# Seven turned block products with wh for three of four pairs of blocks, and wh's pieces made in the first mixing layer

## The chip, the cores and the metric

The kernel runs on one core of a Trainium2 chip. The metric is the device time of one execution in microseconds: 1596.6 us before, the median of 3 runs (1596.59 to 1599.89).

## What is computed

Four layers work on x, 2048 rows of 512 numbers in f32. Layers 0 and 2 mix: a two-sided discrete Fourier transform of the normalized rows, of which the real part is kept. Layers 1 and 3 are a gated feed-forward block. Each adds to x.

```python
def _A_ref(x, dft_seq_re, dft_seq_im, dft_hid_re, dft_hid_im):
    a = jnp.einsum("bsd,ed->bse", x, dft_hid_re)
    b = jnp.einsum("bsd,ed->bse", x, dft_hid_im)
    y = jnp.einsum("ts,bse->bte", dft_seq_re, a) - jnp.einsum("ts,bse->bte", dft_seq_im, b)
    return y

def _B_ref(x, w_gate, w_up, w_down):
    return (_gelu(x @ w_gate) * (x @ w_up)) @ w_down

x = x + _A_ref(_layernorm(x, axis=-1), A_dft_seq_re, A_dft_seq_im, A_dft_hid_re, A_dft_hid_im)
x = x + _B_ref(_layernorm(x, axis=-1), B_w_gate, B_w_up, B_w_down)
...
```

The kernel multiplies in the other order: first the transform over the sequence (ws), then the one over the 512 columns (wh).

## The kernel before

**Products.** TensorE (PE) takes f32 values as pairs of a high and a low part: ScalarE (ACT) copies the high part (L157), VectorE (DVE) subtracts it for the low part (L159), and `mm3` (L214 to L216) makes three matmuls of 128x512. The parts of the streamed matrices are made on the fly: `take` hands out the next item of a list `items`, and makes parts for up to seven items ahead.

**Fewer products by sums.** A product of 2x2 blocks of matrices is made with seven products instead of eight, from sums and differences of the blocks. That is done for ws, for the gate and up matrices and mostly for the down matrix. Sums are VectorE's work (`plus` L194 and L197, `minus` L190).

**A mixing layer** (`mix`) goes through four blocks of 512 rows. `plan` lists the steps: A11 and A12 of all blocks, then for each block S2 (144 matmuls: three products, for which VectorE makes three sums and three low parts for each k), wh products, S4 (96 matmuls) and the other wh products. With wh a block has eight products of 12 matmuls (`hid_groups`): two before S4 (EARLY_HID), six behind it (MID_HID, LATE_HID). Their results lie in four banks, which ScalarE seeds with x and copies out.

**A pair** (`pair_groups`, `pair_product`). Two blocks can share seven products with wh, turned: wh's piece is the stationary operand, and the results are columns. Then wh stands as seven pieces (`whd`), made from whc by `weight_steps`: sums and four `divide` steps, with VectorE, ScalarE and stores on GpSimd's (POOL) queue. Each of the seven products P1 to P7 has four values of k, and six matmuls for each. The blocks' sums are differences of their columns: `arrived` (P7 and P5), `pair_sums` (P6 and P3). Results are added on VectorE and turned by `turned_into` (a transpose L815 and a sum L197 into a wide tile that holds x). The first block of a pair has 2 products before S4 and 6 behind it, the second also; the remaining twelve (PAIR_REST: P6, P5 and P3) come later. Before, only blocks 2 and 3 of layer 2 are a pair, and its rest stands in layer 3, one product at a time beside the up products (`spare`, `beside_mix`). wh's pieces are made in the second half of layer 1.

**Chores.** Work for later layers (norms, weights' pieces) is cut into small steps, spread over the wh products: `chores_at` says which block has which.

**Order.** The order of each engine's instructions follows from the program's order, priorities and a scheduler; each engine then takes its instructions in that order. Slots `s` are 98 tiles of 128x512 in SBUF, to which 8 more are lent from the wide tiles `wide` and `xwide` while these are free (`lend`, `reclaim`); `p` are 8 banks of PSUM.

Of the kernel before, what the change touches and what calls it, by code (L numbers as in the profile page):

```python
# [17 lines left out]
ND = D // P  # L18
# [25 lines left out]
MIXED = 4  # L44
PAIRED = {2: (2, 3)}
LATER = 3
LET = 5
# [6 lines left out]
def fnet_geglu(ctx: ExitStack, tc: tile.TileContext, x_in, ws, wh, wgu, wdn, wdc, whc, out):  # L54
# [409 lines left out]
    )  # L464
    PAIR_REST = [(name, k) for name in ("P6", "P5", "P3") for k in (2, 3, 0, 1)]
# [12 lines left out]
    def plan(layer):  # L478

        fore, steps = FORE[layer], []  # L480
        steps += [(b, "A11") for b in range(fore)] + [(b, "A12") for b in range(fore)]
        for b in range(NB):
            if b >= fore:
                steps += [(b, "A11"), (b, "A12")]
            if b in PAIRED.get(layer, ()):
                n = PAIRED[layer].index(b)
                steps += [(b, "S2"), (b, PAIR_EARLY[n]), (b, "S4"), (b, PAIR_LATE[n])]
            else:
                steps += [(b, "S2"), (b, EARLY_HID), (b, "S4"), (b, MID_HID), (b, LATE_HID)]
        return steps  # L490
# [23 lines left out]
    def mix_items(layer):  # L514
# [3 lines left out]
        for b, what in plan(layer):  # L518
# [17 lines left out]
            elif what == "S4":  # L536
                for i, k in skewed(2):
                    if layer and (b, k) in wss and i == 0:
                        raw(plain, wss[b, k][3])
                    elif i == 0:  # L540
                        raw(make_s4(layer, b, k), a12[k])
                    else:
                        raw(plain, a22[k])
            elif b in PAIRED.get(layer, ()):
# [277 lines left out]
    def mix(layer):  # L822
        hid, sums, chores, hid_left = {}, {}, [], [0]

        def chores_at(b):
            if b == NB - 3:
                norms, others = block_steps(layer + 1, 0)
                later.update(norms=norms[NT:], fetches=others[:ND], others=others[ND:])
                return norms[:NT]
            if b == NB - 2:  # L830
# [35 lines left out]

        paired = PAIRED.get(layer, ())
        xu, xv, pair_banks, kept_p, pair_wide, late_v, sums_due = {}, {}, {}, {}, {}, {}, []

        def arrived(b, m, c):  # L870
            if b not in paired:
                return
            t = cs.pop((m, c))
            if b == paired[0]:
                (xv if m else xu)[c] = t
                cs["P2" if m else "P1", c] = t
                return
# [19 lines left out]

        def pair_wide_load(n):
# [3 lines left out]
            moved(pair_wide[n], xs[layer, paired[n]], lambda v, rows: nc.sync.dma_start(v, rows))  # L902

        def pair_out(n):
            moved(pair_wide[n], xs[layer + 1, paired[n]], lambda v, rows: nc.gpsimd.dma_start(rows, v))

# [153 lines left out]
        def s2(b):  # L1060
            last = b == NB - 1
            if b == 0:
                lend("z")
# [39 lines left out]
        def s4(b):  # L1103
            last = b == NB - 1
            if b == NB - 4:
                sb.reclaim("z")
            if paired and b == paired[0] - 1:
                sb.reclaim("x")
# [160 lines left out]
    def geglu(w, layer):  # L1269
# [517 lines left out]
```

## Time and profile before

| | |
|---|---|
| median of 3 runs | 1596.6 us |
| profiled execution, span | 1596.4 us |
| instructions | 22835 |
| DMA | 431.75 MB, mean 270 GB/s |
| matmuls of L214, L215, L216 | 2312 each |

The span lies 0.2 us below the median, so sums are made on the span. In the trace, the blocks of layer 0 follow each other from 97 us on, about 76 us each, until 402 us; layer 1 lasts until 802 us, layer 2's blocks begin at 889 us, and layer 3 at about 1174 us. A busy PE in the profile is modelled, so what it can lose is read from the starts of matmuls, and from what they wait for. The numbers 0 to 3 of layers and blocks are the code's.

### The profile page before, as it was taken

To read this page: it belongs to the slowest core of one execution; us is meant where nothing else is said; L and a number is where in the kernel's file an instruction comes from. 1 tells how busy PE (TensorE), PEld (TensorE's weight loads), DVE (VectorE), ACT (ScalarE), POOL (GpSimd) and SP (SyncE) were. 2 spreads that over 40 slices of the span, in tenths; PEclk is the share of its full clock that TensorE was granted. 3 is DMA by queue.
4 is the path that set the end of the run, shared out by engine and by line. 5 is a ranking of instruction groups with operands and counts; after the bars stand their busy time and mean duration, and the time that the engine had idled before them with its cause. 6 is when DMAs were issued, how large, how long until landed. Compare 5 with 4: busy or idle time off the path is not lost.

```text
span 1596.4 us, 22835 instructions
## 1 busy us (share of the span) xinstructions
PE 1590.0 (100%) x6984; PEld 1311.2 (82%) x6984; DVE 1169.2 (73%) x2030; ACT 891.6 (56%) x1731; POOL 294.9 (18%) x505
## 2 busy tenths in 40 slices
PE   9999999999999999999999999999999999999999
PEld 6888888888888888888888888888888888888887
DVE  7997878888689794665879767778895557844574
ACT  8955465755777553666657535556553565333460
POOL 4122111251456101330040000101301000000000
PEclk9999999999999999999999999999999999999999
DMA  9898888996988999997895876878978958895445
GB/s 352 289 336 310 292 319 274 359 315 201 324 317 321 285 319 295 332 363 239 288 303 177 272 248 215 272 239 256 254 258 275 284 182 253 300 291 175 133 145 158
DMA packets 244058, 431.75 MB, mean 270 GB/s; under 512 B 29344, under 2 KB 68512, under 8 KB 242912
## 3 DMA queue, kind: packets, MB, share of 16 engines
q1 hardware_dynamic: 214128, 337.21, 66.2%
q0 software_dynamic: 27120, 90.99, 15.7%
q10 hardware_dynamic: 2688, 2.10, 0.5%
q8 instruction: 55, 0.90, 0.2%
q14 instruction: 67, 0.55, 0.1%
HBM read 341.31 MB, written 88.87 MB: 269 GB/s over the span
## 4 chain that ended last, share of the span: by engine, by line
PE 91%; issue 3%; DMA 3%; DVE 2%; ACT 1%; POOL 1%; SPq 0%; DVEq 0%; POOLq 0%; ACTq 0%
PE p L214 30%; PE p L215 30%; PE p L216 30%; DVE s L159 1%; DMA s<-ws 1%; DMA s<-t 1%; PE p L1010 0%; ACT s L157 0%; DMA s<-x 0%; DVE s L190 0%; POOL rstd L628 0%; DMA wide<-ws 0%; POOL s L754 0%; DVE xwide L190 0%; POOL wb L323 0%
## 5 line engine op out<-in xcount | busy, mean ns | idle before, releaser
L215 PE MATMUL p<-s,s 128*128 128x512 f32 x2312 | 897.4, 389 | 0.8 <-DVE s L159 0.8
L216 PE MATMUL p<-s,s 128*128 128x512 f32 x2312 | 891.8, 389 | 0.0
L214 PE MATMUL p<-s,s 128*128 128x512 f32 x2312 | 860.4, 389 | 0.3 <-ACT p L208 0.2
L157 ACT ACTIVATE s<-s 128x512 fp32r<-128x512 f32 (+1 forms) x855 | 481.3, 608 | 265.3 <-DVE s L190 73.6
L159 DVE TENSOR_TENSOR s<-s,s 128x512 fp32r<-128x512 f32 (+1 forms) x855 | 536.6, 661 | 115.3 <-ACT s L157 97.7
L215 PEld LDWEIGHTS p<-s,s 128*128 128x128 f32 x2312 | 433.9, 188 | 91.9 <-DVE s L159 1.9
L214 PEld LDWEIGHTS p<-s,s 128*128 128x128 f32 x2312 | 433.9, 188 | 91.7 <-ACT p L208 0.9
L216 PEld LDWEIGHTS p<-s,s 128*128 128x128 f32 x2312 | 434.0, 188 | 90.3
L194 DVE TENSOR_TENSOR s<-s,p 128x512 f32<-128x512 f32 x201 | 135.6, 682 | 160.3 <-PE p L216 138.1
L190 DVE TENSOR_TENSOR s<-s,s 128x512 f32<-128x512 f32 (+1 forms) x413 | 243.5, 609 | 6.2 <-DMA s<-ws 2.8
L201 ACT ACTIVATE s<-p 128x512 f32<-128x512 f32 x232 | 134.3, 593 | 108.0 <-PE p L216 106.3
L1264 ACT ACTIVATE s<-s 128x512 f32<-128x512 f32 x84 | 52.8, 628 | 46.4 <-DVE s L194 45.5
L628 POOL TENSOR_SCALAR rstd<-rstd 128x1 f32<-128x1 f32 x40 | 19.6, 489 | 237.2 <-ACT s L627 229.3
L1264 ACT ACTIVATE s<-p 128x512 f32<-128x512 f32 x28 | 16.7, 598 | 83.2 <-PE p L216 81.6
L323 POOL DMA_DIRECT2D wb<-s x84 | 46.1, 550 | 92.7 <-ACT s L157 70.5
L159 DVE TENSOR_TENSOR s<-xwide,s 128x512 fp32r<-128x512 f32 (+1 forms) x52 | 34.9, 679 | 29.2 <-ACT s L157 29.2
L651 ACT ACTIVATE s<-s,shift,rstd 128x512 f32<-128x512 f32 x59 | 47.5, 812 | 15.2 <-DVE shift L618 8.5
L1280 DVE TENSOR_TENSOR s<-s,p 128x512 f32<-128x512 f32 x56 | 38.2, 683 | 23.7 <-PE p L216 23.7
L197 DVE TENSOR_TENSOR s<-s,s 128x512 f32<-128x512 f32 (+1 forms) x71 | 42.8, 609 | 11.9 <-DMA s<-ws 10.4
L208 ACT ACTIVATE p<-p 128x512 f32<-128x512 f32 x56 | 32.6, 585 | 24.0 <-PE p L216 23.7
L157 ACT ACTIVATE s<-xwide 128x512 fp32r<-128x512 f32 (+1 forms) x52 | 31.6, 622 | 25.5 <-DVE xwide L194 18.2
L1201 POOL DMA_DIRECT2D wc<-s x42 | 30.5, 728 | 70.8 <-ACT s L157 61.9
(104 smaller groups left out, 614.9 us busy)
## 6 DMA issues: line engine op xcount, KB each, us to landing
s<-ws SPq DMA_DIRECT2D x404, 256.0 KB, 5.2
s<-wb SPq DMA_DIRECT2D x294, 256.0 KB, 5.2
s<-wc SPq DMA_DIRECT2D x182, 256.0 KB, 4.7
wb<-s POOLq DMA_DIRECT2D x98, 256.0 KB, 4.9
s<-wh SPq DMA_DIRECT2D x84, 256.0 KB, 5.3
s<-x SPq DMA_DIRECT2D x55, 256.0 KB, 5.4
wc<-s POOLq DMA_DIRECT2D x49, 256.0 KB, 5.3
xwide<-ws SPq DMA_DIRECT2D x37, 256.0 KB, 5.3
```

The costliest lines, as they stand in the source:

```text
L157: newest["ACT"] = nc.scalar.activation(hi, src, AF.Copy)
L159: newest["DVE"] = nc.vector.tensor_tensor(lo, src, f32(hi), op=ALU.subtract)
L190: nc.vector.tensor_tensor(out, a, b, op=ALU.subtract)
L194: bank_read["DVE"] = nc.vector.tensor_tensor(out, a, b, op=ALU.add)
L197: nc.vector.tensor_tensor(out, a, b, op=ALU.add)
L201: bank_read["ACT"] = nc.scalar.activation(v, src, AF.Copy)
L214: nc.tensor.matmul(ps, ah, bh, start=start, stop=False, skip_group_check=True)
L215: nc.tensor.matmul(ps, ah, bl, start=False, stop=False, skip_group_check=True)
L216: newest["PE"] = nc.tensor.matmul(ps, al, bh, start=False, stop=stop, skip_group_check=True)
L323: nc.gpsimd.dma_start(a, f32(t))
L651: nc.scalar.activation(z, x, AF.Identity, bias=shift, scale=rstd)
L1264: nc.scalar.activation(t, g, AF.Gelu_apprx_tanh)
```

## The change

Three of the four pairs of blocks in the two mixing layers now take seven turned products: blocks 2 and 3 of layer 0, and both pairs of layer 2; blocks 0 and 1 of layer 0 keep eight products each. Four `weight_steps` for wh's pieces move from layer 1 into the chores of blocks 0 and 1 of layer 0. The rest of layer 0's pair stands beside the up products of layer 1, that of layer 2's second pair as before in layer 3; that of layer 2's first pair (`PAIR_REST`) is a step of its own behind block 1, ahead of S2 of block 2. In layer 2, where block 0 is paired, the wide tiles aren't lent in the blocks, and the norms of the first four row tiles for layer 3 move from block 1 to block 2.

```diff
-PAIRED = {2: (2, 3)}
-LATER = 3
+PAIRED = {0: ((2, 3),), 2: ((0, 1), (2, 3))}
+LATER = 4
...
+    def paired_with(layer, b):
+        return next((p for p in PAIRED.get(layer, ()) if b in p), ())
...
-            if b in PAIRED.get(layer, ()):
-                n = PAIRED[layer].index(b)
+            if paired_with(layer, b):
+                n = paired_with(layer, b).index(b)
                 steps += [(b, "S2"), (b, PAIR_EARLY[n]), (b, "S4"), (b, PAIR_LATE[n])]
+                if n and b < NB - 1:
+                    steps.append((b, PAIR_REST))
...
         def chores_at(b):
+            jobs = []
+            if layer == 0 and paired and b < ND // 2:
+                two = [weight_steps(k, whc, whd) for k in range(2 * b, 2 * b + 2)]
+                jobs = [two[0][0]] + [run for i, (_, runs) in enumerate(two) for run in [load for load, _ in two[i + 1:]] + runs]
+            return jobs + next_layer(b)
+
+        def next_layer(b):
             if b == NB - 3:
                 norms, others = block_steps(layer + 1, 0)
-                later.update(norms=norms[NT:], fetches=others[:ND], others=others[ND:])
-                return norms[:NT]
+                later.update(norms=norms if b in paired else norms[NT:], fetches=others[:ND], others=others[ND:])
+                return [] if b in paired else norms[:NT]
...
         def pair_groups(b, groups):
-            n, early = paired.index(b), groups in PAIR_EARLY
+            pair_now[0] = by_pair[b]
+            n, early = by_pair[b].index(b), groups in PAIR_EARLY
+            if groups is PAIR_REST:
+                for i in range(len(groups)):
+                    pair_rest(i)
+                    step()
...
+                return
             if early:
                 chores.extend(chores_at(b))
-                hid_left[0] = 16 if n else 8
-                if not n:
-                    fetch_sums(paired[1])
-                pair_wide_load(n)
+                hid_left[0] = 16 if n and b == NB - 1 else 20 if n else 8
+                if b + 1 < NB:
+                    fetch_sums(b + 1)
+                pair_wide_load(b, n)
             for i, (name, k) in enumerate(groups):
-                if not early and not n and i == 2:
-                    s2_seeded(paired[1])
+                if not early and b + 1 < NB and i == (4 if n else 2):
+                    s2_seeded(b + 1)
...
-                spare.extend(lambda i=i: pair_rest(i) for i in range(len(PAIR_REST)))
+                if b == NB - 1:
+                    spare.extend(lambda i=i: pair_rest(i) for i in range(len(PAIR_REST)))
...
+            if layer and first_paired == 0 and b == FORE[layer] - 1:
+                sb.reclaim("x")
+                sb.reclaim("z")
...
-            if b == 0:
+            if b == 0 and first_paired:
                 lend("z")
                 lend("x")
...
-            run = spare.pop(0) if spare and (layer > 1 or n >= 1) else None
+            run = spare.pop(0) if spare and (w == 0 or n >= 1) else None
...
-            jobs = [weight_steps(k, whc, whd) for k in range(ND)]
+            jobs = [] if 0 in PAIRED else [weight_steps(k, whc, whd) for k in range(ND)]
```

**Layer 2, the end of block 1's S4.** VectorE's rows before, as built: the last two sums from S4's banks `p3` and `p6`, then sums of ws for S2 of block 2 (L197, L190) and the parts of wh products (L185, L159).

```order
L194 TENSOR_TENSOR s61_11180<-s61_11180,p3_10942 128x512
L194 TENSOR_TENSOR s31_11182<-s31_11182,p6_10943 128x512
L197 TENSOR_TENSOR s57_11508<-s79_11506,s57_11508 128x512
L197 TENSOR_TENSOR s20_11518<-s71_11516,s20_11518 128x512
L197 TENSOR_TENSOR s47_11560<-s86_11558,s47_11560 128x512
L197 TENSOR_TENSOR s78_11609<-s55_11607,s78_11609 128x512
L185 SCALAR_TENSOR_TENSOR s6_11555<-s61_11180,s15_11554 128x512
L190 TENSOR_TENSOR s79_11506<-s5_11510,s79_11506 128x512
```

VectorE's rows of the change at the same place: four sums from S4's banks (L194) with the pair's differences between and behind them.

```order
L194 TENSOR_TENSOR s55_11465<-s11_11202,p2_10966 128x512
L194 TENSOR_TENSOR s25_11467<-s0_11204,p5_10967 128x512
L190 TENSOR_TENSOR s21_11469<-s20_10802,s55_11465 128x512
L190 TENSOR_TENSOR s35_11472<-s23_10804,s25_11467 128x512
L190 TENSOR_TENSOR s55_11465<-s55_11465,s96_11245 128x512
L190 TENSOR_TENSOR s25_11467<-s25_11467,s78_11247 128x512
L159 TENSOR_TENSOR s50_11478<-s21_11469,s22_11477 128x512
L159 TENSOR_TENSOR s47_11484<-s35_11472,s53_11483 128x512
L194 TENSOR_TENSOR s11_11202<-s11_11202,p1_10968 128x512
L194 TENSOR_TENSOR s0_11204<-s0_11204,p0_10969 128x512
L190 TENSOR_TENSOR s20_10802<-s55_11465,s20_10802 128x512
L190 TENSOR_TENSOR s23_10804<-s25_11467,s23_10804 128x512
```

The sums of ws for the next block's S2, which stood right behind S4's last sums, now stand some forty rows further on, behind the differences and sums of the pair.

**Layer 0, from S4 of block 2 to S2 of block 3.** VectorE's rows before: the last sums of S4, sums of ws, and the sums of 256 that belong to a piece of the gate and up matrices.

```order
L194 TENSOR_TENSOR s26_3363<-s26_3363,p1_3102 128x512
L194 TENSOR_TENSOR s88_3365<-s88_3365,p2_3103 128x512
L197 TENSOR_TENSOR s20_3719<-xwide_1457,s20_3719 128x512
L197 TENSOR_TENSOR s22_3729<-s62_3727,s22_3729 128x512
L197 TENSOR_TENSOR s48_3461<-s27_3462,s48_3461 128x256
L190 TENSOR_TENSOR s68_3460<-s79_3459,s27_3462 128x256
L185 SCALAR_TENSOR_TENSOR s15_3766<-s26_3363,s85_3765 128x512
```

VectorE's rows of the change there, from the last two sums of S4 on.

```order
L194 TENSOR_TENSOR s31_3488<-s31_3488,p1_3233 128x512
L745 STREAM_TRANSPOSE wide_3648<-s55_3912 128x16x32
L194 TENSOR_TENSOR s79_3490<-s79_3490,p2_3234 128x512
L197 TENSOR_TENSOR s85_3838<-s17_3836,s85_3838 128x512
L159 TENSOR_TENSOR s90_3853<-s24_3834,s35_3852 128x512
L197 TENSOR_TENSOR s3_3848<-s22_3846,s3_3848 128x512
L197 TENSOR_TENSOR s72_3591<-s18_3592,s72_3591 128x256
L190 TENSOR_TENSOR s89_3590<-s34_3589,s18_3592 128x256
L185 SCALAR_TENSOR_TENSOR s48_3879<-s31_3488,s80_3878 128x512
```

A transpose of the norms and a part for a wh product have come between the same kinds of rows; behind them PE has 36 matmuls with wh ahead of block 3's S2, where it had 72.

**Layer 2, the end of block 3's S4.** VectorE's rows of the change, with the bank that the first product of layer 3 takes over, `p1`.

```order
L194 TENSOR_TENSOR s55_13195<-s0_12906,p7_12630 128x512
L194 TENSOR_TENSOR s22_13197<-s25_12908,p6_12631 128x512
L190 TENSOR_TENSOR s61_13223<-s42_12860,s73_13161 128x512
L159 TENSOR_TENSOR s9_13232<-s96_13129,s56_13231 128x512
L159 TENSOR_TENSOR s58_13242<-s73_13161,s14_13241 128x512
L190 TENSOR_TENSOR s12_13199<-s8_12371,s55_13195 128x512
L194 TENSOR_TENSOR s0_12906<-s0_12906,p1_12632 128x512
```

PE's rows there: the last matmuls of S4, and behind them the first product of layer 3, into `p1`.

```order
L215 MATMUL p7_12630<-s52_13094,s88_9478 128x512
L216 MATMUL p7_12630<-s92_13093,s88_9478 128x512
L215 MATMUL p6_12631<-s52_13094,s88_9478 128x512
L216 MATMUL p6_12631<-s92_13093,s88_9478 128x512
L214 MATMUL p1_13381<-s5_12997,s18_13249 128x512
L215 MATMUL p1_13381<-s7_12998,s18_13249 128x512
```

VectorE's rows before at that place begin with sums from `p2` and `p0`.

```order
L194 TENSOR_TENSOR s33_12740<-s33_12740,p2_12466 128x512
L190 TENSOR_TENSOR s42_13029<-s42_13029,s93_12781 128x512
L194 TENSOR_TENSOR s47_12742<-s47_12742,p0_12467 128x512
L159 TENSOR_TENSOR s65_13134<-s23_12965,s20_13133 128x512
L159 TENSOR_TENSOR s76_13168<-s30_12910,s38_13167 128x512
```

Before, the other two banks of S4 had been read some 20 matmuls earlier; now all four end together, and the sum that frees `p1` is VectorE's seventh row behind them.

More of the change, by code (lines that the diff above doesn't have):

```diff
@@ L464, in fnet_geglu @@
     )
-    PAIR_REST = [(name, k) for name in ("P6", "P5", "P3") for k in (2, 3, 0, 1)]
+    PAIR_REST = tuple((name, k) for name in ("P6", "P5", "P3") for k in (2, 3, 0, 1))
     def pair_items(names):
         return [(F32R, (piece(whd[k], FORM[name]),), make_pair(name, k), (name, k)) for name, k in names]
+    def paired_with(layer, b):
+        return next((p for p in PAIRED.get(layer, ()) if b in p), ())
     def skewed(n):
@@ L543, in mix_items @@
                         raw(plain, a22[k])
-            elif b in PAIRED.get(layer, ()):
+            elif paired_with(layer, b):
                 items.extend(pair_items(what))
@@ L865, in hid_groups @@
                     x_out(layer, b * NT + i, ps)
-        paired = PAIRED.get(layer, ())
-        xu, xv, pair_banks, kept_p, pair_wide, late_v, sums_due = {}, {}, {}, {}, {}, {}, []
+        paired = {b for p in PAIRED.get(layer, ()) for b in p}
+        first_paired = min(paired, default=NB)
+        by_pair = {b: p for p in PAIRED.get(layer, ()) for b in p}
+        xu, xv, pair_banks, kept_p, pair_wide, late_v, sums_due, pair_now = {}, {}, {}, {}, {}, {}, [], [()]
         def arrived(b, m, c):
@@ L873, in arrived @@
             t = cs.pop((m, c))
-            if b == paired[0]:
+            if b == by_pair[b][0]:
                 (xv if m else xu)[c] = t
@@ L896, in pair_sums, with pair_wide_load @@
             cs["P6", c], cs["P3", c] = u, v
-        def pair_wide_load(n):
+        def pair_wide_load(b, n):
             pool = tpool if n else upool
@@ L901, in pair_wide_load @@
             pair_wide[n] = pool.tile([P, NT * D], F32, name="wide" if n else "xwide")
-            moved(pair_wide[n], xs[layer, paired[n]], lambda v, rows: nc.sync.dma_start(v, rows))
+            moved(pair_wide[n], xs[layer, b], lambda v, rows: nc.sync.dma_start(v, rows))
         def pair_out(n):
-            moved(pair_wide[n], xs[layer + 1, paired[n]], lambda v, rows: nc.gpsimd.dma_start(rows, v))
+            moved(pair_wide[n], xs[layer + 1, pair_now[0][n]], lambda v, rows: nc.gpsimd.dma_start(rows, v))
         LAST = {"P1": 3, "P2": 1, "P7": 3, "P4": 1, "P6": 1, "P5": 1, "P3": 1}
@@ L959, in pair_groups @@
         def pair_groups(b, groups):
-            n, early = paired.index(b), groups in PAIR_EARLY
+            pair_now[0] = by_pair[b]
[4 more added lines that the diff above has]
+                    step()
+                    for _ in range(-(-len(chores) // hid_left[0]) if chores else 0):
+                        chores.pop(0)()
+                    hid_left[0] -= 1
+                return
             if early:
                 chores.extend(chores_at(b))
-                hid_left[0] = 16 if n else 8
-                if not n:
-                    fetch_sums(paired[1])
-                pair_wide_load(n)
+                hid_left[0] = 16 if n and b == NB - 1 else 20 if n else 8
+                if b + 1 < NB:
+                    fetch_sums(b + 1)
+                pair_wide_load(b, n)
             for i, (name, k) in enumerate(groups):
-                if not early and not n and i == 2:
-                    s2_seeded(paired[1])
+                if not early and b + 1 < NB and i == (4 if n else 2):
+                    s2_seeded(b + 1)
                 pair_product(name, k)
@@ L1104, in s4 @@
             last = b == NB - 1
-            if b == NB - 4:
+            if b == NB - 4 and first_paired:
                 sb.reclaim("z")
-            if paired and b == paired[0] - 1:
+            if b == first_paired - 1:
                 sb.reclaim("x")
```

## Prediction

> **What bounds the kernel now.** First the page's busy line and the chain of work that ended last: is one engine the wall, or several by turns?
>
> ```profile
> PE 1590.0 (100%) x6984; PEld 1311.2 (82%) x6984; DVE 1169.2 (73%) x2030; ACT 891.6 (56%) x1731; POOL 294.9 (18%) x505
> PE 91%; issue 3%; DMA 3%; DVE 2%; ACT 1%; POOL 1%; SPq 0%; DVEq 0%; POOLq 0%; ACTq 0%
> ```
>
> TensorE holds 91% of the chain. A busy share of 100% is not yet proof, so the second view is the list of waits, for PE alone:
>
> ```profile
> PE p L1693 <- POOL ident masks.py:199: 1.4, 1, 1.4
> PE p L215 <- DVE s L159: 0.8, 1, 0.8
> PE p L214 <- ACT p L208: 0.2, 1, 0.2
> ```
>
> After the start PE waits 1.0 us in all. The kernel is as long as its matmuls, at the spacing that the third view, the timeline, shows. Two rows of an undisturbed stretch, 32 matmuls apart (start, length, engine):
>
> ```profile
> 398.27 0.39 PE L214 MATMUL p<-s,s 128*128 128x512 f32 x1
> ...
> 405.52 0.39 PE L216 MATMUL p<-s,s 128*128 128x512 f32 x1
> ```
>
> 7.25 us in 32 steps is 0.2266 us for a matmul. A matmul less is worth that, **as long as nothing else ends later**. So the fourth view is how full the other engines are just where the change works: layer 0 from block 2 to block 3, layer 2 from block 1 to block 2, and the end of layer 2. Columns: stretch, its length, then busy time and count of PE, PEld, DVE, ACT, POOL.
>
> ```profile
> 287.43:309.19 21.76, 21.76 (x98) 18.02 (x96) 14.57 (x25) 15.55 (x34) 8.29 (x14) 1.00 1.03 385
> 309.19:325.51 16.32, 16.32 (x74) 13.51 (x72) 16.32 (x31) 9.69 (x18) 4.54 (x10) 1.00 1.04 394
> 325.51:358.15 32.64, 32.64 (x146) 27.03 (x144) 25.15 (x43) 17.47 (x33) 18.45 (x34) 1.00 1.03 301
> 1026.52:1042.84 16.32, 16.32 (x73) 13.51 (x72) 16.32 (x28) 9.68 (x20) 3.29 (x6) 1.00 0.67 221
> 1042.84:1075.48 32.64, 32.64 (x145) 27.03 (x144) 23.89 (x40) 17.91 (x38) 1.56 (x5) 1.00 0.70 222
> 1165.24:1185.00 19.76, 19.54 (x86) 15.72 (x85) 19.30 (x33) 15.15 (x28) 0.00 (x0) 1.00 0.64 212
> 602.00:800.00 198.00, 198.00 (x875) 163.97 (x874) 129.17 (x216) 113.64 (x229) 37.34 (x59) 1.00 0.91 303
> ```
>
> The second and the fourth row are the 72 matmuls with wh that follow S4 of a block. There **VectorE is busy for 16.32 of 16.32 us**: it makes S2's sums and parts for the next block ahead, because S2 itself leaves it little room. These matmuls are its breathing space, and the change shortens it and fills it.
>
> **What VectorE's work costs.** The last place where before has VectorE full, 1165 to 1185 us, gives every duration needed:
>
> ```profile
> 1166.12 0.69 DVE L194 TENSOR_TENSOR s<-s,p 128x512 f32<-128x512 f32 x1 [0.46 <-PE p L216]
> ...
> 1168.87 0.39 PE L215 MATMUL p<-s,s 128*128 128x512 f32 x1
> 1169.09 0.39 PE L216 MATMUL p<-s,s 128*128 128x512 f32 x1
> 1169.13 0.69 DVE L190 TENSOR_TENSOR s<-s,s 128x512 f32<-128x512 f32 x1
> 1169.32 0.61 PE L214 MATMUL p<-s,s 128*128 128x512 f32 x2
> 1169.52 0.58 ACT L208 ACTIVATE p<-p 128x512 f32<-128x512 f32 x1 [0.84 <-PE p L216]
> 1169.73 0.69 DVE L159 TENSOR_TENSOR s<-s,s 128x512 fp32r<-128x512 f32 x1
> 1170.01 1.14 ACT L157 ACTIVATE s<-s 128x512 fp32r<-128x512 f32 x2
> 1170.15 0.50 PE L214 MATMUL p<-s,s 128*128 128x512 f32 x1 [0.22 <-ACT p L208]
> 1170.33 0.69 DVE L190 TENSOR_TENSOR s<-s,s 128x512 f32<-128x512 f32 x1
> 1170.49 0.39 PE L215 MATMUL p<-s,s 128*128 128x512 f32 x1
> ```
>
> Rows of 512 on VectorE stand 0.60 us apart when packed (1169.13, 1169.73, 1170.33), though one lasts 0.69; two on ScalarE 0.52 (1.14 less one of 0.62). A reader of a bank starts 0.43 after the start of the matmul that ends it (1169.09 to 1169.52), and PE goes on 0.05 after the reader's end (1170.10 to 1170.15). Rows of 256 take 0.34 by the timeline at 122.58:
>
> ```profile
> 122.58 0.42 DVE L190 TENSOR_TENSOR xwide<-s,xwide 128x256 f32<-128x256 f32 x1
> 122.92 0.68 DVE L159 TENSOR_TENSOR s<-s,s 128x512 fp32r<-128x512 f32 x1
> ```
>
> **The change part by part.** *Removed*: two blocks need 2 x 96 matmuls with wh; as a pair, 7 x 4 products of 6 are 168. Two pairs more: 48 matmuls less, 48 x 0.2266 = **10.9 us**. [...]
>
> *Added on VectorE*: for a pair 28 parts of products instead of 16, 16 differences (P7, P5 and the two pair sums, four each), 8 sums and 8 turned pieces of two rows: 52 rows, 104 in all, 104 x 0.60 = 62 us. ScalarE gets 8 rows more. Spread over 1596 us with VectorE at 73% this would cost nothing. It isn't spread.
>
> *Moved*: the four jobs for wh's pieces, each 4 sums and a part of 256 and three parts of 512 on VectorE (5 x 0.34 + 3 x 0.60 = 3.5 us), 3 loads and 7 stores, go from layer 1 into the wh products of blocks 0 and 1 of layer 0. Where they came from VectorE had 129 of 198 us to do and PE none to wait: nothing is won there. Where they go costs what the places 1 and 2 below show. Their stores queue on POOL, which is below 60% busy in every stretch above. The 12 products of the rest of layer 0's pair stand in layer 1 beside the up products, as layer 2's do today in layer 3: nothing, since no run of rows there is short in the count below. LATER and the norms' places: nothing for PE, their VectorE rows are in the counts. Layer 2 loses the 8 lent slots in blocks 0 and 1: from nothing to two loads more on the path, 10 us by the row of loads below; I take nothing, since the stretch at 1042 moves only 222 GB/s, and keep the 10 for the range.
>
> ```profile
> s<-ws SPq DMA_DIRECT2D x404, 256.0 KB, 5.2
> ```
>
> *The added rows at their places*. In the new order the waits of every row of VectorE and ScalarE lead back to the last matmul that it needs, and forward to the first matmul that needs it. Where a run of rows must lie between two matmuls, the rows' packed time is set against the matmuls between (time before in brackets):
>
> 1. layer 0, S2 of block 1 ends (183, 203): VectorE 0.1 over; ScalarE 11 rows, 5.7 us in 20 matmuls, 4.5: 1.2 over
> 2. layer 0, S4 of block 2 begins (279): ScalarE 6 rows, 3.1 in 5 matmuls, 1.1: 2.0
> 3. layer 0, block 2 to 3 (301): VectorE 39 rows, 22.4 in 70 matmuls, 15.9: **6.5**
> 4. layer 0, end of S4 of block 3 (363): 20 rows, 11.2 in 31 matmuls, 7.0: 4.2
> 5. layer 2, block 0 to 1 (935): 28 rows, 16.9 in 67 matmuls, 15.2: 1.7
> 6. layer 2, block 1 to 2 with the rest of its pair (997 to 1042): 33 rows, 19.9 in 69, 15.7: 4.2; then 59 rows, 35.5 in 127, 28.8: **6.7**
> 7. layer 2, in block 2 (1058, 1082): 0.7 and 0.4
> 8. layer 2, S4 of block 3 ends (1150): 32 rows, 19.3 in 69 matmuls, 15.6: 3.6
>
> Together 31.3 us in 11 runs. To each comes the passing to and fro: 0.43, 0.05 and 0.08 (0.69 less 0.60), 0.56: 6.2 us. **37.5 us**. The same count over before finds one place after the start, 1163 to 1177 us, with 0.5 us; the fence above shows 0.38 us lost there at 1170.15 (0.61 after the row at 1169.54) and 0.11 at 1170.49. So the count reads true, and it is a floor: it takes VectorE as packed. In the fullest window, 1165 to 1185, VectorE was 19.30 of 19.76 busy, 2.3% short; of the 125 us of VectorE rows in the places 3 to 8 that is 2.9.
>
> Sum against the profiled execution: span 1596.4 - 10.9 - 0.5 (the old place, which place 8 replaces) + 37.5 + 2.9 = 1625.4; the median lies 0.2 above the span: **1625.6 us**.
>
> **The rivals.** *A, faster*: VectorE and ScalarE do their rows ahead, no run is tight, and the 10.9 us are kept: 1586. This is decided at place 6: the 94 rows between the end of block 1's S4 and the middle of block 2's S2 take 56.6 us, and would have to be at most 76 to fit into the 203 matmuls there, 46.0 us. For it: 427 us of VectorE's span are idle. Against it: the row that opens the run reads a bank that S4 has just ended, and the engine takes its rows in the order that is written. [...]
>
> *B, slower by less*: the runs are there, but about half of their excess is lost inside each other, as a stall in one place lets VectorE run ahead into the next: 1600 to 1616. Against it: the runs don't overlap in matmuls.
>
> *C, slower by more*: inside the runs VectorE isn't packed, since its parts wait for ScalarE's halves and sums for loads. Six large runs with a landing of 5.2 us each: 1626 + 31 = 1657. For it is the chain of waits of before, early in layer 2 (start, length, what):
>
> ```profile
> 872.47 5.11 DMA wide<-ws
> ...
> 887.30 3.79 DMA s<-ws
> ...
> 892.31 4.82 DMA s<-ws
> ...
> 906.93 0.50 PE p L215
> ```
>
> Three loads follow each other there. Against it: all of them together cost PE the 0.8 us of its list of waits.
>
> *D*, that the products aren't fewer, is excluded: the new order has 6912 matmuls where the old has 6960.
>
> **How the numbers follow.** Forecast 0.81, A 0.03, B 0.07, C 0.09. The range takes in the 10 us for slots and the lower half of C, and below the forecast the lag taken away with place 2's and the small ones: 1616 to 1646. A measurement of this kernel tells 0.2%, about 3 us, from no change. Faster 0.02, same 0.01, slower 0.97.
>
> **What would show it.** In the profile after: PE's waits list led by VectorE, with some 30 us and more, at L214 and L215, behind L194 and L159 rows; PE's instructions down by 48, VectorE's up by 104; windows with VectorE at 97% or more and PE with gaps around 300, 365, 1000 to 1045 and 1150 us; the rest of layer 0's pair in layer 1 without a gap. It is wrong if PE's spacing stays 0.2266 through block 1 to block 2 of layer 2, or if the long gaps have loads as their releaser.

## The result, and the profile after

The changed kernel takes 1679.32 us (median of 4 runs, 1676.59 to 1684.29) against 1597.32 us before (4 runs, 1596.59 to 1599.89): **5.1% slower**, ratio 1.051 with the interval 1.0481 to 1.0539. Forecast were 1625.6 us, 1616 to 1646. The sign was right; the loss is 82 us where 29 were forecast, and lies outside the range. The profiled execution took 1681.55 us, its span is 1679.8 us.

First the page of after, busy line and chain, to be set against the two lines of before:

```profile
PE 1614.1 (96%) x6936; PEld 1311.4 (78%) x6936; DVE 1231.8 (73%) x2134; ACT 900.8 (54%) x1739; POOL 292.6 (17%) x505
PE 71%; DMA 10%; DVE 10%; issue 3%; ACT 3%; SPq 1%; POOL 1%; DVEq 0%; ACTq 0%; POOLq 0%
```

TensorE has its 48 matmuls less (6984 to 6936), VectorE its 104 rows more (2030 to 2134), ScalarE 8 more. PE's share of the chain fell from 91% to 71%. What it lost went mainly to two: VectorE, from 2% to 10%, as forecast in kind, and DMA, from 3% to 10%, which was not forecast. PE's busy time is higher with fewer matmuls; that is the first sign that some of them went slower.

The second view is PE's list of waits in after (us in total, times, longest), 1.0 us before once the start is left out:

```profile
PE p L215 <- DVE s L159: 16.9, 14, 4.3
PE p L214 <- ACT s L157: 15.5, 12, 3.1
PE p L214 <- DVE s L194: 12.9, 4, 7.6
PE p L214 <- ACT p L208: 5.1, 2, 4.6
PE p L214 <- ACT s L201: 3.7, 4, 1.7
PE p L214 <- ACT s L183: 2.9, 3, 1.3
PE p L214 <- DMA s<-wq: 2.6, 1, 2.6
```

VectorE leads with 29.8 us at L159 and L194, as forecast; ScalarE (ACT) follows with 27.2. But these seven rows hold 59.6 us, and the kernel lost 83.4 us of span on top of the 10.9 us that it should have won. The rest is in no row of this list, because in it PE isn't waiting. The third view shows it: windows of 2 us of after, around its longest wait (stretch, length, busy time and count of PE, PEld, DVE, ACT, POOL, then the granted clock, the busy share of the DMA engines and GB/s):

```profile
400.00:402.00 2.00, 1.29 (x6) 0.75 (x4) 2.00 (x5) 0.79 (x2) 0.00 (x0) 1.00 0.93 284
402.00:404.00 2.00, 0.00 (x0) 0.00 (x0) 2.00 (x5) 1.68 (x3) 0.00 (x0) 1.00 0.90 306
404.00:406.00 2.00, 0.00 (x0) 0.00 (x0) 2.00 (x4) 0.00 (x0) 0.00 (x0) 0.64 0.62 202
406.00:408.00 2.00, 0.00 (x0) 0.00 (x0) 2.00 (x5) 0.00 (x0) 0.00 (x0) 0.50 0.38 126
408.00:410.00 2.00, 1.12 (x3) 0.93 (x4) 2.00 (x5) 1.74 (x3) 0.00 (x0) 0.50 0.22 66
410.00:412.00 2.00, 2.00 (x6) 1.55 (x5) 2.00 (x5) 0.25 (x2) 0.56 (x1) 0.50 0.00 0
412.00:414.00 2.00, 2.00 (x6) 1.57 (x5) 2.00 (x5) 0.43 (x1) 0.00 (x0) 0.50 0.34 131
414.00:416.00 2.00, 2.00 (x8) 1.60 (x8) 2.00 (x4) 0.40 (x1) 0.00 (x0) 0.80 0.00 0
```

This is the end of S4 of layer 0's block 3, place 4 of the prediction. VectorE is full in every row. PE stands still for 7.6 us, three whole rows and parts of two, and while it stands the granted clock falls from 1.00 to 0.50. It stays at 0.50 for some 6 us after PE has work again.

The timeline of after at the same place (start, length, engine, line, in brackets the wait and what ended it):

```profile
400.67 0.39 PE L215 MATMUL p<-s,s 128*128 128x512 f32 x1
400.90 0.39 PE L216 MATMUL p<-s,s 128*128 128x512 f32 x1
...
407.55 0.69 DVE L190 TENSOR_TENSOR s<-s,s 128x512 f32<-128x512 f32 x1
...
408.15 0.68 DVE L194 TENSOR_TENSOR s<-s,p 128x512 f32<-128x512 f32 x1
408.88 0.79 PE L214 MATMUL p<-s,s 128*128 128x512 f32 x1 [7.60 <-DVE s L194]
409.48 0.63 PE L215 MATMUL p<-s,s 128*128 128x512 f32 x1
409.90 0.63 PE L216 MATMUL p<-s,s 128*128 128x512 f32 x1
410.33 0.63 PE L214 MATMUL p<-s,s 128*128 128x512 f32 x1
```

PE's starts stand 0.23 us apart ahead of the wait (400.67 to 400.90) and 0.42 to 0.43 behind it (409.48 to 409.90 to 410.33). So the starts give the whole account. Over all matmuls of after from 20 us on, the spacing less 0.2267 us adds up, by its size:

| spacing | before, us | after, us |
|---|---|---|
| over 0.6 us: waits | 1.4 | 66.5 |
| 0.4 to 0.6: steps of 0.427 at half the clock | 0.3 | 21.7 |
| smaller: steps of about 0.236 and 0.335, nearly all right behind a wait | 0.6 | 9.2 |
| 48 matmuls less | | -10.9 |

The difference is 97.4 - 2.3 - 10.9 = 84.2 us; the span grew by 83.4. Nothing of any size is left over.

The 66.5 us of waits, put beside the prediction's places (its count with 0.56 us for each run, and what the starts of matmuls show there):

| place | counted, us | measured, us |
|---|---|---|
| 1 layer 0, S2 of block 1 ends | 2.4 | 4.4 |
| 2 layer 0, S4 of block 2 begins | 2.6 | 2.5 |
| 3 layer 0, block 2 to 3 | 7.1 | 6.3 |
| 4 layer 0, end of S4 of block 3 | 4.8 | 7.8 |
| 5 layer 2, block 0 to 1 | 2.3 | 1.6 |
| 6 layer 2, block 1 to 2 | 12.0 | 9.5 |
| 7 layer 2, in block 2 | 2.2 | 5.5 |
| 8 layer 2, S4 of block 3 ends | 4.2 | 4.1 |
| together | 37.5 | 41.7 |
| elsewhere | 0 | 24.8 |

In after these waits begin at 191, 195, 213 and 216 us (place 1), 296 and 298 (2), 326 to 335 (3), 401 (4), 1006 and 1011 (5), 1073 to 1108 (6), 1138, 1141 and 1177 to 1186 (7) and 1244 (8). Which wait belongs to which place follows from the order of the blocks. The three from 1177 on, 3.4 us, stand at the beginning of block 3's S2; without them place 7 has 2.1 us and the sum is 38.3.

Where the prediction looked, its sum was right to about a tenth. The single places miss by up to 3.3 us, to both sides, so a part of that closeness is luck. The prediction missed two things: 24.8 us of waits at places that it didn't count, and 31 us behind the waits. Two of the uncounted places show what they are made of. The chain of after at 476 us, early in layer 1 (start, length, what):

```profile
471.16 1.02 SPq L251
...
472.24 1.00 SPq L251
...
473.27 1.08 SPq L251
...
477.38 1.81 DMA s<-x
479.19 0.15 ACT s L630
...
479.90 0.49 ACT p L208
480.40 0.04 issue
480.44 0.79 PE p L214
```

SP issues loads of x in pieces of 64 KB (L251), five of them at about 1 us each; then a piece lands, ScalarE makes a norm from it (L630), and only then comes the seeding of a bank (L208) that stands behind the norm in ScalarE's queue and for which PE waits, 4.75 us. No VectorE row is in this chain. The other place is the end of S2 in layer 2's block 3, where PE waits 3.22 us at 1213. The timeline of after shows what ended this wait, a ScalarE row that had itself stood 4.21 us for a load of ws:

```profile
1216.08 1.67 ACT L157 ACTIVATE s<-s 128x512 fp32r<-128x512 f32 x3 [4.21 <-DMA s<-ws]
1216.76 0.65 PE L214 MATMUL p<-s,s 128*128 128x512 f32 x1 [3.06 <-ACT s L157]
```

That load was issued at 1202.33, right behind the last piece of the pair's x. The chain of after goes through this piece and a later load of ws, to PE's next wait, 1.49 us at 1225.6:

```profile
1200.92 13.38 DMA wide<-x
...
1214.37 8.56 DMA s<-ws
```

The piece of x takes 13.38 us into its wide tile, and the load of ws behind it about 13.7, where the median of a 256 KB load of ws is 5.0 in the same profile.

### The profile page after: what moved, and what is told of

The parts are those of the page before. It is cut to its first block, busy times and chain, and to the rows that moved or that the text cites. A ratio compares the mean times of both kernels' runs of the same rounds, so it can differ in the third digit from the quotient of the medians.

```text
span 1679.8 us, 22819 instructions
## 1 busy us (share of the span) xinstructions
PE 1614.1 (96%) x6936; PEld 1311.4 (78%) x6936; DVE 1231.8 (73%) x2134; ACT 900.8 (54%) x1739; POOL 292.6 (17%) x505
## 4 chain that ended last, share of the span: by engine, by line
PE 71%; DMA 10%; DVE 10%; issue 3%; ACT 3%; SPq 1%; POOL 1%; DVEq 0%; ACTq 0%; POOLq 0%
PE p L215 24%; PE p L214 24%; PE p L216 23%; DMA s<-ws 5%; DVE s L159 4%; DVE s L190 2%; DMA s<-x 1%; DMA wide<-x 1%; ACT s L157 1%; DVE s L194 1%; DVE s L197 1%; DMA s<-t 1%; SPq L251 1%; DMA xwide<-wdc 1%; PE p L1034 1%
## 5 line engine op out<-in xcount | busy, mean ns | idle before, releaser
L157 ACT ACTIVATE s<-s 128x512 fp32r<-128x512 f32 (+1 forms) x918 | 517.2, 608 | 350.5 <-DVE s L190 92.6
L159 DVE TENSOR_TENSOR s<-s,s 128x512 fp32r<-128x512 f32 (+1 forms) x918 | 576.4, 663 | 135.9 <-ACT s L157 118.9
L190 DVE TENSOR_TENSOR s<-s,s 128x512 f32<-128x512 f32 (+1 forms) x459 | 274.8, 620 | 27.4 <-DMA s<-ws 20.3
L194 DVE TENSOR_TENSOR s<-s,p 128x512 f32<-128x512 f32 x224 | 150.8, 682 | 192.9 <-PE p L216 145.6
L197 DVE TENSOR_TENSOR s<-s,s 128x512 f32<-128x512 f32 (+1 forms) x85 | 52.0, 623 | 12.2 <-DMA s<-ws 6.8
L1307 DVE TENSOR_TENSOR s<-s,p 128x512 f32<-128x512 f32 x56 | 38.3, 683 | 25.0 <-PE p L216 24.7
L633 POOL TENSOR_SCALAR rstd<-rstd 128x1 f32<-128x1 f32 x40 | 15.7, 393 | 230.8 <-ACT s L632 229.9
L919 POOL DMA_DIRECT2D x<-wide x12 | 7.8, 659 | 248.2 <-DVE wide L197 176.5
L208 ACT ACTIVATE p<-p 128x512 f32<-128x512 f32 x56 | 32.6, 583 | 25.1 <-PE p L216 23.0
L745 DVE STREAM_TRANSPOSE wide<-s 128x512 f32<-128x512 f32 x32 | 22.4, 706 | 23.8 <-ACT s L656 19.1
L1307 DVE TENSOR_TENSOR s<-s,s 128x512 f32<-128x512 f32 x56 | 38.5, 687 | 1.2
```

What stands on the lines that cost most here:

```text
L157: newest["ACT"] = nc.scalar.activation(hi, src, AF.Copy)
L159: newest["DVE"] = nc.vector.tensor_tensor(lo, src, f32(hi), op=ALU.subtract)
L190: nc.vector.tensor_tensor(out, a, b, op=ALU.subtract)
L194: bank_read["DVE"] = nc.vector.tensor_tensor(out, a, b, op=ALU.add)
L197: nc.vector.tensor_tensor(out, a, b, op=ALU.add)
L1307: nc.vector.tensor_tensor(t, t, v, op=ALU.mult)
```

## The experiments

Theory 1 going in: the added VectorE rows at the counted places cause the waits, and the half clock and late loads come on top. The rivals were that the loss belongs to one pair alone, to the slots, to GpSimd's or SP's queue, or to the loads. Ratios are against before as measured together with each run: 1598.35 us for the first four experiments, 1598.20 for the next four, 1599.48 for the last two. "After" is the changed kernel; its 1679.32 us were measured apart from these runs, beside 1597.32 for before, so differences against it are good to some 2 us more or less.

**One pair at a time.** After, without layer 0's pair (`p2only`), and after, without layer 2's first pair (`p0only`). What hangs on a pair goes with it: `p2only` makes wh's pieces in layer 1 again, and `p0only` lends the slots in layer 2 again.

```diff
-PAIRED = {0: ((2, 3),), 2: ((0, 1), (2, 3))}
+PAIRED = {2: ((0, 1), (2, 3))}
```

> The two pairs of layer 2 alone; layer 0 as before, wh's pieces made in layer 1 again. 24 matmuls less than before, 5.4 us. Theory 1 (waits, the steps at half clock behind them and the short steps add up place by place, each layer for itself): layer 2 of the changed kernel lost 47 us against a spacing of 0.2266, so 1597 - 5.4 + 45 = about 1637 us, with the same waits as there at S4's end of block 1 (4.7 us) and of block 3 (4.1 us). Rival (the counted runs of rows are the whole cost): 22.6 us of waits in layer 2, 1614 us.

```diff
-PAIRED = {0: ((2, 3),), 2: ((0, 1), (2, 3))}
+PAIRED = {0: ((2, 3),), 2: ((2, 3),)}
```

> Blocks 2 and 3 of layer 0 as a pair, with wh's pieces made in blocks 0 and 1 of layer 0; layer 2 with one pair as before. 24 matmuls less than before. Theory 1: layers 0 and 1 of the changed kernel lost 49 us, so 1597 - 5.4 + 49 = about 1641 us. Rival (the counted runs alone): 17 us of waits, 1608 us. If both single parts together lose much less than the changed kernel's 82 us, the layers disturb each other.

Measured: 1634.19 us (1.0222, 1.0202 to 1.0242) and 1649.22 us (1.0316, 1.0295 to 1.0337). That is 35.8 and 50.9 us more than before; together 86.7, and the whole change costs 82.0. Each of the two is known to some 3 us, so within the noise the loss is the sum of two local ones, and each pair alone loses much more than the 5.4 us that its 24 matmuls are worth. Rival B, which had one stall make room for the next, has no support here. The waits stay where they were: `p2only` has the 1.21 and 3.45 us at the end of block 1's S4 and the 4.09 us at the end of block 3's, to the hundredth as in after; `p0only` has the 4.50 us between blocks 2 and 3 of layer 0, 7.97 at the end of block 3's S4 and 4.80 at 476 us.

**The lent slots.** The kernel before, with the eight lent slots taken back ahead of layer 2's blocks:

```diff
+            if layer and b == FORE[layer] - 1:
+                sb.reclaim("x")
+                sb.reclaim("z")
...
-            if b == 0:
+            if b == 0 and layer == 0:
```

> The kernel before, with the 8 lent slots taken back ahead of layer 2's blocks, as the change does; nothing else. If the missing slots delay loads in blocks 0 and 1 of layer 2: up to two landings of 5 us, 1602 to 1607 us, with waits between 890 and 1040 us. If slots aren't short there: within 0.2% of before.

Measured: 1597.64 us (0.9995, 0.9985 to 1.0004). The slots cost nothing in the kernel before; whether they would beside the fuller runs of the changed one, this doesn't show.

**The clock behind a wait.** The kernel before, with two waits made by hand in layer 3, where nothing else is tight: the first part of a product is given a chain of VectorE rows to wait for, whose sum is zero.

```diff
+HELD_UP = {1: 1, 5: 5}
...
+                if i in HELD_UP:
+                    t, wait = at0[i], sb.get()
+                    plus(t, t, ps)
+                    minus(wait, t, t)
+                    for _ in range(HELD_UP[i]):
+                        minus(wait, wait, wait)
+                    first = vs[0][0]
+                    nc.vector.tensor_tensor(first, f32(first), wait, op=ALU.subtract)
```

> The kernel before with two waits put in by hand ahead of groups of 12 matmuls near the end of layer 3, where nothing else waits: a chain of 4 and one of 8 dependent VectorE rows, about 3.0 and 5.8 us. Theory 1 (a wait of over about 2.4 us is followed by a stretch in which the granted clock is 0.5): 6 to 12 matmuls 0.427 us apart behind each, 1.2 to 2.4 us more than the wait itself, and dips of the clock that before hasn't. Rival (the slow steps in the changed kernel come from operands that arrive late one by one): matmuls 0.2266 us apart right behind the waits, no dip. The time is before's plus 9 us, and 3 to 4 us more by theory 1.

Measured, in one run: 1612.65 us, 14.3 more than before. The windows of this kernel around the first wait, in the columns above:

```profile
1574.00:1576.00 2.00, 0.74 (x4) 0.28 (x2) 0.00 (x0) 0.00 (x0) 0.00 (x0) 1.00 0.97 350
1576.00:1578.00 2.00, 0.00 (x0) 0.00 (x0) 1.94 (x3) 0.00 (x0) 0.00 (x0) 0.81 1.03 337
1578.00:1580.00 2.00, 0.45 (x1) 0.46 (x2) 1.42 (x3) 0.00 (x0) 0.00 (x0) 0.50 1.14 337
1580.00:1582.00 2.00, 2.00 (x6) 1.52 (x6) 0.00 (x0) 0.00 (x0) 0.00 (x0) 0.50 0.71 258
1582.00:1584.00 2.00, 2.00 (x7) 1.52 (x6) 0.00 (x0) 0.00 (x0) 0.00 (x0) 0.50 0.70 177
1584.00:1586.00 2.00, 2.00 (x10) 1.68 (x9) 0.69 (x1) 0.00 (x0) 0.00 (x0) 0.98 0.91 348
```

The waits were 4.97 and 6.03 us, the first longer than meant. Behind them stand 9 and 12 matmuls 0.427 us apart, and apart from ten VectorE rows for the two chains the kernel has the rows and loads of before. So a wait is enough for the half clock to follow; no late load or crowded queue is needed. The two waits are 11.0 us and the steps of 0.4 to 0.6 us 5.9 more: these waits cost about half as much again as they last.

**The differences taken away.** After, without the differences of P7, P5 and the pair sums that VectorE makes in L896 to L909; P7's are copies on ScalarE:

```diff
-                minus(v, xu[c], t)
+                nc.scalar.activation(v, xu[c], AF.Copy)
...
-                minus(v, v, late_v[c])
...
-            minus(u, cs["P5", c], u)
-            with behind("DVE"):
-                nc.vector.scalar_tensor_tensor(v, v, -1.0, u, op0=ALU.mult, op1=ALU.subtract)
```

> The changed kernel without 36 of its VectorE rows: the differences for P5, P6 and P3 are left out (their operands stay as they are) and that for P7 is a ScalarE copy, in all three pairs. Matmuls, loads and stores as in the changed kernel. Theory 1 (VectorE's runs of rows are the largest cause, and each wait of over 2.4 us costs 1 to 2.6 us of half clock more): the counted runs fall from 37.5 to 26.5 us, most at S4's end of block 3 in layers 0 (4.8 to 0.6) and 2 (4.2 to 1.5), where the half clock goes too: 1679 - 11 - 5 = about 1663 us; the waits on loads stay. Rival (loads, slots or queues are the cause and VectorE only waits with them): 1675 to 1680 us.

Measured: 1668.02 us (1.0436, 1.0406 to 1.0466), 11.3 us below after. VectorE has 48 rows less (2134 to 2086), 16 for each of the three pairs. The expectation had counted 36 rows, and 1668 lies between its two forecasts. The two ends of S4 lose about what the count has for them: 4.09 us becomes 1.0 in layer 2, and 7.76 becomes 3.97 in layer 0. But the 3.13 us at 270, 5.13 at 476 and the waits early in S2 stay, and others come, such as 2.88 at 351. The 32 of them that the change had added, a third of its 104, and the old pair's 16 are worth 11 us, so VectorE's rows are a cause, and not the only one.

**The differences moved to GpSimd.** After, with three of four of these rows, 36, on the engine that has the most room, 17% busy:

```diff
-                minus(v, xu[c], t)
+                nc.gpsimd.tensor_tensor(v, xu[c], t, op=ALU.subtract)
...
-                minus(v, v, late_v[c])
+                nc.gpsimd.tensor_tensor(v, v, late_v[c], op=ALU.subtract)
...
-            minus(u, cs["P5", c], u)
+            nc.gpsimd.tensor_tensor(u, cs["P5", c], u, op=ALU.subtract)
```

> The changed kernel with 36 of the pairs' 48 differences on GpSimd instead of VectorE. Theory 1: VectorE's counted runs fall to 30.8 us, so 1679 - 7 - 3 = about 1669 us, if a difference of 128x512 takes GpSimd less than about 1 us. Rival: GpSimd is slower, its stores queue behind the differences, and the products wait for it instead: 1680 us and more.

Measured: 1689.80 us (1.0572, 1.0541 to 1.0603), 10.5 above after; the rival was right. The group of one of these lines in that kernel (busy time, mean ns of one):

```profile
L896 POOL TENSOR_TENSOR s<-s,s 128x512 f32<-128x512 f32 x12 | 23.5, 1965 | 153.9 <-DVE s L197 60.0
```

A difference takes 1.97 us there (1.67 and 1.72 on the two other lines), against 0.69 for such a row on VectorE. The runs are chains from one bank to the next matmul, and a row that is three times as long lengthens its chain. That isn't all: VectorE's own rows got longer beside GpSimd's. The timeline of this kernel at the end of S4 in layer 2's block 3:

```profile
1252.11 6.32 POOL L900 TENSOR_TENSOR s<-s,s 128x512 f32<-128x512 f32 x4
1255.49 6.85 DVE L159 TENSOR_TENSOR s<-s,s 128x512 fp32r<-128x512 f32 x4
```

Four rows of L159 take 6.85 us here, 1.71 each, where one lasts 0.69 elsewhere. In the whole kernel 26 VectorE rows last 1.2 to 1.8 us, all of them beside a GpSimd difference; in after none does. How much of the 10.5 us each of the two effects costs isn't separated.

**Later work for layer 3** (`p0only` with another LATER), and **norms in another block** (`p0only` with the first four norms for the next layer moved from block 1's chores to block 2's):

```diff
-LATER = 4
+LATER = 9
```

> The pair of layer 0 alone (as in p0only, 1649 us), with the loads of x for the norms of layer 1's second half begun five slow steps later (LATER 9 for 4). Theory 2 (the wait of 4.8 us at 476 us, which no run of rows explains, comes from ScalarE standing behind a norm whose x load is still to come, with the bank's seed queued behind it): this wait and its 2.2 us of half clock go, 1649 - 7 = 1642 us, or 1644 with the 2 us that a new counted run at 1332 us costs. Rival (the rest of the pair itself takes too long there): the wait stays, 1649 us.

```diff
-                later.update(norms=norms if b in paired else norms[NT:], fetches=others[:ND], others=others[ND:])
-                return [] if b in paired else norms[:NT]
+                later.update(norms=norms if paired else norms[NT:], fetches=others[:ND], others=others[ND:])
+                return [] if paired else norms[:NT]
```

> The pair of layer 0 alone, with the first four norms for layer 1 moved from block 1's chores to block 2's. Theory 2 (the wait of 3.3 us for wh's piece at 271 us comes from GpSimd's queue: a norm's small steps wait for x, and stores behind them free no slots for the next loads): the wait at 271 us goes with its half clock, 4 us; the counted runs grow by 3.2 us, so the time stays near 1648 us while the place changes. Rival (the piece is late because loads in all are too many there): the wait at 271 us stays, and the time is 1652 us or more.

The second edit moves the norms in layer 2 as well. Measured: 1652.49 us (1.0339, 1.0309 to 1.0369) and 1660.40 (1.0388, 1.0342 to 1.0435), against 1649.22 for `p0only` (1.0295 to 1.0337). In both the wait that was aimed at went: the 4.8 us at 476 with LATER 9, and 3.32 us at 271 shrank to 0.68 without the norms. And in both others came: 1.88 us at 648, 2.57 at 681 and some 9 us around 1390 in the first (6.19, 0.93 and 2.26); in the second 1.50, 3.54 and 4.03 between 323 and 333, 3.27 at 371 and 5.73 at 1192. So these two waits hang on the norms and their loads of x that stand there, and nothing is won by moving them. Which queue hands the wait on at 271 us, ScalarE's or GpSimd's, isn't shown; it also shrinks, to 1.20 us, with the loads of the next experiment. Why the other waits come isn't shown either.

**The pairs' loads of x in whole rows.** After loads a pair's x into the wide tiles through `moved`, in an order of columns that cuts it into short packets. Here the rows are loaded as they lie, 2 KB each, and so x is added at other places than it belongs:

```diff
-            moved(pair_wide[n], xs[layer, b], lambda v, rows: nc.sync.dma_start(v, rows))
+            for i in range(NT):
+                nc.sync.dma_start(pair_wide[n][:, i * D:(i + 1) * D], rows(layer, b * NT + i))
```

> The changed kernel with the pairs' loads of x as whole rows of 2 KB instead of pieces of 512 bytes: the same bytes and the same order on PE, VectorE and ScalarE, a quarter of the packets; x is added at other places than it belongs. Theory 2 (the waits at 272, 1146 and 1213 us, 2.7, 1.4 and 3.2 us, which no run of rows explains, are loads that land late, because the many small packets of a pair's x fill the queues when each pair block begins): these waits and their half clock go, 1679 - 7 - 3 = about 1669 us. Rival (those loads are late since their slots come free late): 1677 to 1681 us, the waits stay.

Measured: 1665.88 us (1.0422, 1.0404 to 1.0439), 13.4 below after, with the same order on PE, VectorE and ScalarE. The packets' line of before, of after and of this kernel:

```profile
DMA packets 244058, 431.75 MB, mean 270 GB/s; under 512 B 29344, under 2 KB 68512, under 8 KB 242912
```

```profile
DMA packets 249051, 429.66 MB, mean 256 GB/s; under 512 B 29216, under 2 KB 76576, under 8 KB 247904
```

```profile
DMA packets 239834, 429.65 MB, mean 258 GB/s; under 512 B 29216, under 2 KB 64288, under 8 KB 238688
```

12,288 packets under 2 KB are gone, with the same bytes. A stretch in block 0 of layer 2, first in after, then the same 73 matmuls in this kernel (columns as above):

```profile
938.00:960.00 22.00, 18.77 (x74) 14.69 (x73) 17.23 (x29) 6.73 (x11) 0.00 (x0) 0.92 1.07 279
```

```profile
934.38:950.93 16.55, 16.55 (x75) 13.70 (x73) 16.09 (x27) 6.71 (x11) 0.00 (x0) 1.00 0.84 288
```

The busy share of the DMA engines is 1.07 in the first and 0.84 in the second, where PE has no gap. Over the kernel the waits fall from 66.5 to 56.0 us and the half-clock steps from 21.7 to 14.3. The waits of 2.92 us at 949 and 1.35 at 1146 are gone, 3.22 at 1213 is 1.10 and 2.73 at 272 is 1.20; the big ones at the counted places are as they were (4.50, 8.02, 3.45, 4.09).

**Both.** Differences and short packets away:

> Both at once: 36 of the pairs' differences left out as in nodiff (1668 us), and x loaded in whole rows. If the two causes stand beside each other, 1668 - 10 = about 1658 us; if they are the same waits seen twice, about 1668 us. What is left over 1586 us is then the other VectorE and ScalarE rows of the pairs and of wh's pieces (26.5 us counted), and the half clock.

Measured: 1648.79 us (1.0313, 1.0287 to 1.0340), 30.5 below after, where 11.3 and 13.4 are 24.7. Against before as measured beside them, the three lose 69.8, 66.4 and 49.3 us where after loses 82.0: 12.2, 15.6 and 32.7 saved. So the two causes are different ones, and they add; that they save a little more together isn't clear of the noise, since the two runs of this kernel lie 6 us apart. The waits are 40.8 us here, with 12.7 us of half-clock steps and 7.2 of small ones. What is left, 49.3 of the 82.0 us, was not taken away by any run: that it comes from the rest of the rows in the counted runs, the wait of 3.29 us early in layer 1, a few waits on loads, and the clock behind each is read from what released the waits. No kernel with more pairs than before reached the time of before.

## Why the prediction was right and wrong

- **The removed matmuls**: right. 48 are gone, and the spacing of undisturbed ones is 0.227 us as before.
- **The VectorE runs, 37.5 us and 2.9 for lag**: right in mechanism and in sum. 41.7 us are lost at these places, four of the eight within 0.8 us. Place 1 was 2.0 short, place 4 3.0 and place 7 3.3, place 6 2.5 too long, so the sum owes something to luck. That the wait shrinks with the rows was shown at the two ends of S4.
- **Wh's pieces in layer 0's blocks 0 and 1**: priced as part of places 1 and 2, 5.0 us, measured 6.9. Not tried by itself.
- **The slots, nothing**: held in the kernel before; in the changed one not tried.
- **Rival A**: fell; a single pair costs 36 to 51 us.
- **Rival B**: fell, since the two halves of the change add within the noise.
- **"The rest of layer 0's pair in layer 1: nothing"**: wrong. The first wait there is 4.75 us at 475.5, and 0.83, 0.89 and 1.82 us follow at 612 to 682. The step looked at VectorE's runs alone; what came last was an x load behind SP's slow issues and a norm ahead of a seed in ScalarE's queue. That the first of these goes when the later work is moved was shown. The count's check against before already had a sign of this: it found the 0.5 us around 1170, but not before's longest wait, 1.0 us at 906 by the starts, which stands behind loads of ws in the chain that the prediction prints. "The count reads true" held for runs of rows alone.
- **"The sum" with a wait priced at its own length**: this is the step that failed most. The sum has no term for what follows a wait: steps at half the clock and small steps, over the whole kernel 21.7 and 9.2 us. The waits made by hand, 4.97 and 6.03 us with 9 and 12 matmuls 0.427 us apart behind them, showed that the half clock needs no other cause than a wait.
- **Rival C, given 0.09**: partly true. It had six loads landing late inside the large runs; what happened is that 24.8 us of waits stood outside the counted runs, and a part of these led to loads and to queues behind them. The change's own loads, in short packets, are worth 13.4 us, and the large waits that went with them (2.92 us at 949, 1.35 at 1146) stand outside the counted places. That they would crowd the others wasn't asked: their bytes were looked at (222 GB/s in the stretch), not their packets.

By terms, in the spans: forecast +29.0, of it -11.4 for what is removed, +37.5 and +2.9 for waits. Measured +83.4: -10.9, and 2.3 less of before's own losses, +41.7 of waits where counted, +24.8 elsewhere, +21.7 for the clock, +9.2 for small steps, 84.2 together.

The range failed for the same reason: its upper end took in ten us for slots, which came out at nothing, and half of C, but had no term that grows with every wait.

## What to carry to other kernels

Count the rows of the second engine between the matmul whose end frees them and the matmul that needs them, place by place; in sum that was right to about a tenth here, where the shares over the whole kernel said nothing. Then price each wait of TensorE above 3.5 us with the 1.2 to 2.6 us of slow steps that followed each of 22 such waits here, remember that 7 of 10 between 2.2 and 3.5 us were followed by some too, and ask of every moved load what packets it has and what stands behind it in its queue. A change that removes 0.2267 us a matmul pays only while no run comes out longer than its cover.

## What the runs showed that was not expected

**How long the waits were that the half clock followed.** Taking all waits of these kernels (all but before and `b_nolend`) that have no other within 10 us: of 22 above 3.5 us, each is followed by 6 to 13 matmuls 0.427 us apart, 1.2 to 2.6 us in all; of 10 between 2.2 and 3.5, 7 are; of 24 below, 2. Short ones near each other can add up, and the same pair does so or not: 1.46 and 1.00 us, 2 us apart, at 296 us of after, are followed by none, and at 295 us of `p0only` by 7. All records of the granted clock in after are 1.0 or 0.5. Taken as one of these two, by the windows above the clock is at half for (0.19 x 2 + 0.5 x 6 + 0.02 x 2) / 0.5 = 6.8 us around the first hand-made wait, and (0.36 x 2 + 0.5 x 8 + 0.2 x 2) / 0.5 = 10.2 us around the 7.76 us one. The trace of after has ten such falls of the clock before its end: six of 3.41 us, three of 6.83 and one of 10.24. All ten begin on one grid of 3.413 us: those at 274.87, 339.72 and 404.58 us, for instance, each stand 19 steps of it apart.

These falls begin at no fixed distance from their wait: 2.77 us after the last start ahead of it at 272.10 us, 4.20 after the one at 475.47. That could be why the same wait counts once and not another time; this is the author's guess, and it wasn't tried. A wait of 2.73 us was enough at 272 us of after, where 6 steps of 0.427 us follow (3 of the 5 waits between 2.2 and 3.0 are followed by some), and one of 3.27 us at 371 us of `p0norms` wasn't.

**Small steps behind a wait.** Behind a wait, also without a fall of the clock, a few of the next starts stand about 0.236 or 0.335 us apart instead of 0.227; over after this is 9.2 us, 8.6 of them within 25 starts behind a wait. Behind the two hand-made waits it is only 0.05 and 0.11 us, so most of it need not be a price of the restart itself. That operands come one by one there instead is the author's guess; no run shows it.

**Issues on SP aren't always short.** At 471 us of after each issue of a 64 KB piece took about 1 us in the chain above, so five in a row are a wait of their own; the median issue on this line takes 0.42 us in the same kernel. What makes these slow isn't shown. The 64 KB pieces land in a median of 3.8 us over the kernel.
